# Expert weights in one transfer per matrix, ids and gate weights loaded straight into their integer tile

## The chip, the cores and the metric

One core of one Trainium2 chip runs the whole program. The metric is the device time in microseconds (us) of one launch. Lower is better. Weights and constants may be laid out on the host beforehand; that is not in the time.

## The reference

A long convolution by FFT is followed by a two-level mixture of experts. `x` has the shape (8, 5056, 128) and `h` (5056, 128).

```python
Yf = np.fft.rfft(x, n=2*S, axis=1) * np.fft.rfft(h, n=2*S, axis=0)[None]
y = np.fft.irfft(Yf, n=2*S, axis=1)[:, :S, :]          # 8 x 5056 x 128
x = y.reshape(40448, 128)
g_idx = argmax(x @ w_group)                            # 4 groups
e_idx = argmax(xg @ w_expert[g])                       # 4 experts in each
out[tok] = g_w * e_w * (relu(x[tok] @ w1[g, e]) @ w2[g, e])
```

`w1` is 16 matrices of 128 x 1024 and `w2` 16 matrices of 1024 x 128, all float32. Each row of `x` goes through exactly one expert, and its result is multiplied by the two softmax weights of the choice.

## The kernel before, in words

The first part of the program, up to about 545 us, is the convolution: a Fourier transform in two factors, a product with the transformed `h`, and the way back, in three rounds over the batches. The rows that come out are gated and scattered by GpSimd (POOL) into an array in device memory, `srt`, sorted by expert. A row of `srt` has 130 words: 128 values, the token's id as an integer, and its gate weight.

From about 590 us on the experts run in blocks. A block `j` is 512 rows of one expert, and from the block numbers `T0` and `H0` on 384 and 256 rows, for the rests that the experts leave. Blocks up to `NW_MIN` stand straight in the program, woven with the rest of the convolution (`weave`, lists `main` and `steps`); behind them come three chains of blocks under conditions (`ffn_chain`, `ffn_last`), because their number depends on the routing. For the inputs measured these chains hold 11 blocks of 512 rows, 10 of 384 and 9 of 256.

What a block needs is fetched two blocks ahead by SyncE (SP), all on one queue that works in order. `ffn_x(j)` (from L1265) issues five transfers for a block: four of 32 columns each of the sorted rows into `xr`, and a fifth with the two last columns (id and weight). `ffn_w(j)` (from L1305) issues the expert's weights in four pieces of 128 x 512, in the order 0, 2, 1, 3. Pieces 0 and 1 are the halves of `w1`, L1319; pieces 2 and 3 the halves of `w2`, L1321. In `w2` a partition's 512 words come from four rows of 128 words that lie apart in memory. A transfer into a buffer first waits until the last reader of that buffer is done. In the chains, `again` gives block `j` the buffers of block `j - 2`.

Each piece of weights is split into a high part (a cast on ScalarE, ACT, L1330) and a rest (a subtraction on VectorE, DVE, L1331); from `T0` on the rest of piece 3 is computed on POOL. `ffn_turn` (L1338) transposes the rows on DVE (L1346) and then copies ids and weights from the end of `xr` into the tile `ids` (L1348). `ffn_prep_x` splits the transposed rows with the same lines 1330 and 1331. `mm1` (L1393 to L1395) multiplies by `w1` in three products (high by high, low by high, high by low); `relu` and a second split into `h..h` and `h..l` follow (ACT L1398, DVE L1399). `mm2` (L1411 to L1413) multiplies by `w2`. `out_evac` (L1416) and `out_store` (transpose on TensorE, PE, L1427; product with the gate weight on DVE, L1431, into `orow`) bring the rows back, and `scatter_out` (L1464) has POOL send them to the output by id. `keep_ids` (L1479, L1480) copies a chain block's ids and weights into `lids` at the block's end, because the next block, not this one, stores its rows.

`PLAN` sets at which step of a block each of these is issued. For blocks of 256 rows, with four steps, it reads:

```python
HB: [(0, 0, 1), (0, 0, 2), (1, 0, 3), (1, 1, "t"), (2, 1, "x"), (2, 1, 0), (2.5, 0, "s"), (3, 0, "o"), (3, 0, "w")],
```

An entry is the step, the block counted from the present one, and what is done: a number is a piece of weights to split, "t" the turn, "x" the split of the rows, "s" the store, "o" the scatter, "w" the fetch of weights for two blocks ahead. So in step 1 the present block's piece 3 is split (on POOL) and the next block's rows are turned, and in step 2 the next block's rows and its piece 0 are split. The inverse transform of the last round runs beside the first blocks: `side` loads its data with L723 (`zm`) and L730 (`zt`) on the same SP queue.

Of the kernel before, what the change touches and what calls it, by code (L numbers as in the profile page):

```python
# [9 lines left out]
F32 = mybir.dt.float32  # L10
F32R = mybir.dt.float32r
BF16 = mybir.dt.bfloat16
I32 = mybir.dt.int32
# [6 lines left out]
B, S, D = 8, 5056, 128  # L20
# [5 lines left out]
NE, NF = 16, 1024  # L26
# [14 lines left out]
T0, H0 = 1000, 2000  # L41
# [186 lines left out]
def width(j):  # L228

    return BLK if j < T0 else TB if j < H0 else HB  # L230
# [6 lines left out]
class Kernel:  # L237
# [1027 lines left out]
    def ffn_x(self, j):  # L1265
        nc = self.nc
        tab, k = self.entry(j)
        w = width(j)
        T = w // 128
        rb = nc.sync.value_load(  # L1270
            tab[0:1, 2 * k + 1:2 * k + 2], min_val=0, max_val=NR // BLK - 1 if j < T0 else NR - w
        )
        again = self.again(j)
        if again:
            xr = again["xr"]
        elif j > 0:
            xr = self.fx.tile([128, w + 2 * T], F32, name=f"xr{w}", bufs=2)
        else:
            xr = self.cx.tile([128, w + 2 * T], F32, name="xr0", bufs=1)

        def rows(p, c):
            if j < T0:
                return self.srt.rearrange("(b t p) c -> p b t c", p=p, t=w // p)[:, bass.ds(rb, 1), :, c]
            return self.srt[bass.ds(rb, w), c].rearrange("(t p) c -> p t c", p=p).unsqueeze(1)

        parts = [
            (xr[i:i + SQ, 0:w].rearrange("p (t c) -> p t c", c=SQ), rows(SQ, slice(i, i + SQ))) for i in range(0, D, SQ)
        ]
        parts.append((xr[:, w:w + 2 * T].rearrange("p (t c) -> p t c", c=2), rows(128, slice(D, D + 2))))
        for out, src in parts:  # L1290
            ins = nc.sync.dma_start(out=out.unsqueeze(1), in_=src)
            if j < NC:
                k = 0 if j < N0 else 1 if j < NA else 2
                self.join(f"ids{k}", ins)
                for i in range(k + 1, 3):
                    self.free_of(ins, f"scatter_idx{i}")
                self.free_of(ins, "fill")
        ids = again["ids"] if again else self.cp.tile([128, 4, 2], I32, name="ids", bufs=8)[:, 0:T]
        self.blk[j] = dict(ids=ids, xr=xr, T=T, n=w)

    def again(self, j):
# [3 lines left out]
    def ffn_w(self, j, pieces=(0, 2, 1, 3)):  # L1305
        nc, a = self.nc, self.a
        tab, k = self.entry(j)
        e = nc.sync.value_load(tab[0:1, 2 * k:2 * k + 1], min_val=0, max_val=NE - 1)
        w1 = a["moe_w1"].rearrange("g e d f -> d (g e) f")
        w2 = a["moe_w2"].rearrange("g e (f p) d -> p (g e) f d", p=128)  # L1310
        for q in pieces:
            if self.again(j):
                t = self.again(j)[q]
            elif j > 0 or q == 3:
                t = self.fx.tile([128, 512], F32, name=f"wr{width(j)}", bufs=12 if j < T0 else 8)
            else:
                t = self.xt[(0, 2, 1).index(q)]
            if q < 2:
                nc.sync.dma_start(out=t.unsqueeze(1), in_=w1[:, bass.ds(e, 1), q * 512:(q + 1) * 512])  # L1319
            else:  # L1320
                nc.sync.dma_start(  # L1321
                    out=t.rearrange("p (f d) -> p f d", d=D).unsqueeze(1),
                    in_=w2[:, bass.ds(e, 1), q * 4 - 8:q * 4 - 4, :],
                )
            self.blk[j][q] = t

    def split(self, pair, src, w, eng=None):
        nc = self.nc
# [9 lines left out]
    def ffn_turn(self, j):  # L1338
        nc = self.nc
        s = self.blk[j]  # L1340
        n = s["n"]
        if (j, "x") in self.kept:
            t = self.cx.tile([128, W], F32, name="xturn0", tag="zt", bufs=2)[:, 0:n]
        else:
            t = self.fx.tile([128, BLK], F32, name="xturn", bufs=1)[:, 0:n]
        nc.vector.transpose(out=t, in_=s["xr"][:, 0:n])  # L1346
        s["turned"] = t
        nc.vector.tensor_copy(  # L1348
            out=s["ids"], in_=s["xr"][:, n:n + 2 * s["T"]].bitcast(I32).rearrange("p (t c) -> p t c", c=2)
        )  # L1350

    def ffn_prep_w(self, j, q):
        other = self.nc.gpsimd if j >= T0 and q == 3 and j not in (T0, H0) else None
# [121 lines left out]
    def keep_ids(self, j):  # L1475
        nc = self.nc
        s = self.blk[j]
        T = s["T"]
        nc.vector.tensor_copy(out=self.lids[:, 0:T, 0:1], in_=s["ids"][:, :, 0:1])  # L1479
        nc.vector.tensor_copy(out=self.lids[:, 0:T, 1:2].bitcast(F32), in_=s["ids"][:, :, 1:2].bitcast(F32))  # L1480

    def no_rows(self):

# [326 lines left out]
```

## Time and profile before

| what | value |
|---|---|
| runs timed | 3 |
| median, lowest, highest | 1655.28, 1654.49, 1656.99 us |
| the profiled execution's own time | 1650.14 us |
| its span, first to last instruction | 1648.4 us |
| PE busy in the span | 1585.1 us (96%) |
| DVE busy | 1321.2 us (80%) |
| ACT busy | 1030.5 us (63%) |
| POOL busy | 771.6 us (47%) |

Times in the profile count from the first instruction. "SPq" is SP's transfer queue; the duration there is that of issuing, not of the transfer. In a timeline the bracket behind a row says how long the engine stood idle before it and what ended that idle time. Instructions of one engine overlap a little in these rows, since each is shown from its start to the end of its writes; the step from one start to the next is what an instruction costs its engine.

### The profile page before, as it was taken

What the parts mean: (1) busy time and instruction counts of PE and PEld (TensorE: products, weight loads), DVE (VectorE), ACT (ScalarE), POOL (GpSimd) and SP (SyncE); (2) the same over time, 40 slices, a digit from 0 to 9 for tenths busy, and PEclk for the clock granted to TensorE, in tenths of its full rate; (3) what the DMA queues carried; (4) which work ended last, traced back from release to release, by engine and by line L of the source; (5) the groups of instructions that cost most, each with busy time, mean ns of one, the idle gap of its engine ahead of it and who ended that gap; (6) DMA issues with size and microseconds to landing.
All of it is one profiled execution on the core that took longest, in us unless ns stands there. A gap on an engine that the chain in (4) does not pass through costs nothing. (4 is left out here: it accounts for less than half of the span.)

```text
span 1648.4 us, 48424 instructions
## 1 busy us (share of the span) xinstructions
PE 1585.1 (96%) x16432; PEld 1242.0 (75%) x16432; DVE 1321.2 (80%) x2938; ACT 1030.5 (63%) x2286; POOL 771.6 (47%) x742
## 2 busy tenths in 40 slices
PE   8998999989999989999999999999999999999997
PEld 8676856568666647887787777788888878879986
DVE  6654699875788886888887888888898888888887
ACT  5554544544455545666666666677777776767775
POOL 1453234352565653254555555354665654234544
PEclk9999999999999989999999999999999999999999
DMA  7797778979799988666666655658866787556666
GB/s 212 225 279 238 227 246 269 289 232 237 222 292 302 286 218 177 180 182 174 178 180 171 158 140 143 153 155 224 198 172 172 190 199 185 137 129 162 162 163 158
DMA packets 493295, 330.30 MB, mean 200 GB/s; under 512 B 257052, under 2 KB 436769, under 8 KB 493016
## 3 DMA queue, kind: packets, MB, share of 16 engines
q1 hardware_dynamic: 472408, 285.11, 65.3%
q0 software_dynamic: 20608, 41.79, 7.4%
q8 instruction: 136, 2.23, 0.6%
q14 instruction: 143, 1.17, 0.2%
HBM read 230.41 MB, written 96.86 MB: 199 GB/s over the span
## 5 line engine op out<-in xcount | busy, mean ns | idle before, releaser
L877 POOL DMA_INDIRECT srt<-rw,pos x320 | 342.6, 1071 | 333.9 <-DVE y L551 67.0
L1464 POOL DMA_INDIRECT out<-orow,at x176 | 193.0, 1097 | 263.0 <-ACT at L1462 207.7
L551 DVE TENSOR_TENSOR y<-pp,hg 128x768 f32<-128x768 f32 (+1 forms) x120 | 103.3, 861 | 53.8 <-ACT hg L541 33.6
L1464 POOL DMA_INDIRECT out<-orow,sids x92 | 90.6, 985 | 117.5 <-DVE orow L1431 83.8
L611 ACT COPY zs<-pp 128x768 f32<-128x768 f32 (+1 forms) x118 | 85.4, 723 | 56.5 <-PE pp L601 37.7
L601 PE MATMUL pp<-y,cg 64*64 64x384 f32 (+1 forms) x1472 | 113.8, 440 | 4.9 <-DVE rw L994 2.8
L533 PE MATMUL pp<-st,cg 64*64 64x192 f32 (+1 forms) x1556 | 114.5, 404 | 2.9 <-PE pp L601 1.4
L1398 ACT ACTIVATE h0h<-px 128x512 fp32r<-128x512 f32 (+1 forms) x109 | 64.0, 588 | 82.2 <-PE px L1395 82.2
L766 ACT COPY yT<-py 128x474 f32<-128x474 f32 (+1 forms) x96 | 44.4, 515 | 105.0 <-PE py L759 105.0
L551 DVE TENSOR_TENSOR m<-pp,hg 128x768 f32<-128x768 f32 (+1 forms) x120 | 103.0, 859 | 0.0
L446 DVE TENSOR_TENSOR st<-pp,odd 128x320 f32<-128x320 f32 x90 | 43.8, 487 | 71.0 <-ACT odd L445 70.5
L1399 DVE SCALAR_TENSOR_TENSOR h2l<-px,h2h 128x512 fp32r<-128x512 f32 (+1 forms) x112 | 75.4, 673 | 30.6 <-ACT h2h L1398 26.9
L1399 DVE SCALAR_TENSOR_TENSOR h0l<-px,h0h 128x512 fp32r<-128x512 f32 (+1 forms) x109 | 73.3, 672 | 30.7 <-ACT h0h L1398 30.4
L533 PEld LDWEIGHTS pp<-st,cg 64*64 64x64 f32 x1556 | 59.4, 133 | 44.9 <-issue 29.5
L1399 DVE SCALAR_TENSOR_TENSOR h3l<-px,h3h 128x512 fp32r<-128x512 f32 (+1 forms) x111 | 74.6, 672 | 21.7 <-ACT h3h L1398 20.5
L601 PEld LDWEIGHTS pp<-y,cg 64*64 64x64 f32 x1472 | 56.6, 133 | 43.0 <-issue 29.1
L745 PE MATMUL py<-ig,zm 126*64 126x79 f32 x2048 | 82.1, 236 | 5.1 <-DMA zm<-zd 5.1
L585 POOL TENSOR_TENSOR y<-y,m 128x512 f32<-128x512 f32 x40 | 50.9, 1276 | 76.8 <-DVE m L573 42.0
L745 PEld LDWEIGHTS py<-ig,zm 126*64 126x64 f32 x2048 | 73.9, 138 | 17.1 <-issue 11.0
L1398 ACT ACTIVATE h3h<-px 128x512 fp32r<-128x512 f32 (+1 forms) x111 | 65.2, 587 | 31.2 <-PE px L1395 27.5
L1398 ACT ACTIVATE h2h<-px 128x512 fp32r<-128x512 f32 (+1 forms) x112 | 65.7, 587 | 18.8 <-PE px L1395 12.8
L1398 ACT ACTIVATE h1h<-px 128x512 fp32r<-128x512 f32 (+1 forms) x111 | 65.3, 588 | 18.6 <-PE px L1395 16.6
(474 smaller groups left out, 5051.7 us busy)
## 6 DMA issues: line engine op xcount, KB each, us to landing
wr<-in_moe_w SPq DMA_DIRECT2D x373, 256.0 KB
zm<-zd SPq DMA_DIRECT2D x64, 378.0 KB
zd<-zs SPq DMA_DIRECT2D x62, 384.0 KB
cg<-in_c_g SPq DMA_DIRECT2D x102, 224.0 KB
xr<-srt SPq DMA_DIRECT2D x284, 64.0 KB
xt<-in_x SPq DMA_DIRECT2D x82, 160.0 KB
hg<-hd SPq DMA_DIRECT2D x80, 128.0 KB
zd<-zs SPq DMA_DIRECT2D x39, 256.0 KB
```

The costliest lines, as they stand in the source:

```text
L446: nc.vector.tensor_tensor(out=all_st[:, 0:2 * HALF, d], in0=even, in1=odd, op=ALU.add)
L533: nc.tensor.matmul(px[c * 64:c * 64 + 64, b, to], lhsT=k, rhs=data[:, of], start=begin, stop=i == len(steps) - 1 or p == 0 and i == 1, til ...
L551: self.mark["v"] = nc.vector.tensor_tensor(out=t[:, :, 0:w].rearrange("p t (r u d) -> p t r u d", r=2, u=nu), in0=taken(px, part).unsqueez ...
L585: self.mark["v"] = (nc.gpsimd if r == 0 else nc.vector).tensor_tensor(out=y[:, :, 0:w], in0=y[:, :, 0:w], in1=m[:, :, 0:w], op=ALU.add)
L601: nc.tensor.matmul(pz[c][h:h + 64, 0:w], lhsT=wt[c * 64:c * 64 + 64, k + h:k + h + 64], rhs=y[c * 64:c * 64 + 64, part, 0:w], start=part = ...
L611: self.mark["s"] = nc.scalar.copy(out=z[:, 0:n, 0:w], in_=pp[:, 0:n, 0:w])
L745: nc.tensor.matmul(pys[q][c:c + 64, col(n, u)], lhsT=zms[q][:, n % QB, k:k + 64], rhs=self.ig[:, 0:NH], start=n % QB == 0 and u == 0, stop ...
L766: nc.scalar.copy(out=self.yT[:, k:k + QB * c1], in_=pys.pop(q)[:, 0:QB * c1])
L877: ins = self.nc.gpsimd.indirect_dma_start(out=self.srt, out_offset=bass.IndirectOffsetOnAxis(ap=k["pos"][0:p, j:j + 1], axis=0), in_=k["rw ...
L1398: self.mark["s"] = nc.scalar.activation(out=hh, in_=p, func=AF.Relu)
L1399: nc.vector.scalar_tensor_tensor(out=hl, in0=p, scalar=0.0, in1=hh.bitcast(F32), op0=ALU.max, op1=ALU.subtract)
L1464: ins = self.nc.gpsimd.indirect_dma_start(out=self.a["out"], out_offset=bass.IndirectOffsetOnAxis(ap=ids, axis=0), in_=o, in_offset=None, ...
```

## The change

- `w2` is laid out on the host so that each expert's matrix is 128 rows of 1024 words, a row for each partition, as `w1` already was.
- Each matrix of a block is fetched by one transfer into one tile of 128 x 1024, so that a partition gets 4096 bytes in one piece: two transfers a block where there were four. The first is issued where piece 0 was, the second where piece 2 was. Block 0 keeps its four.
- The fifth transfer of `ffn_x` goes straight into the tile `ids`, which has 10 buffers instead of 8, or, in the chains, the buffer of the block three before. The copy in `ffn_turn` is gone.
- `keep_ids` copies ids and weights in one instruction instead of two.

```diff
@@ ffn_x @@
-            xr = self.fx.tile([128, w + 2 * T], F32, name=f"xr{w}", bufs=2)
+            xr = self.fx.tile([128, w], F32, name=f"xr{w}", bufs=2)
...
+        if again is None:
+            ids = self.cp.tile([128, 4, 2], I32, name="ids", bufs=10)[:, 0:T]
+        else:
+            ids = self.blk[j - 3]["ids"] if j - 3 in self.blk and self.again(j - 1) else None
+            if ids is None:
+                ids = self.cp.tile([128, 4, 2], I32, name="ids", bufs=10)[:, 0:T]
...
-        parts.append((xr[:, w:w + 2 * T].rearrange("p (t c) -> p t c", c=2), rows(128, slice(D, D + 2))))
+        parts.append((ids, rows(128, slice(D, D + 2)).bitcast(I32)))
...
-        ids = again["ids"] if again else self.cp.tile([128, 4, 2], I32, name="ids", bufs=8)[:, 0:T]
@@ ffn_w @@
-        w2 = a["moe_w2"].rearrange("g e (f p) d -> p (g e) f d", p=128)
+        w = [a["moe_w1"].rearrange("g e d f -> d (g e) f"), a["moe_w2"].rearrange("e p f -> p e f")]
         for q in pieces:
...
-            if q < 2:
-                nc.sync.dma_start(out=t.unsqueeze(1), in_=w1[:, bass.ds(e, 1), q * 512:(q + 1) * 512])
...
+            elif q % 2 == 0:
+                if self.again(j):
+                    t = self.again(j)["w", q]
+                else:
+                    t = self.fx.tile([128, 1024], F32, name=f"wr{width(j)}", bufs=6 if j < T0 else 4)
+                nc.sync.dma_start(out=t.unsqueeze(1), in_=w[q // 2][:, bass.ds(e, 1)])
+                self.blk[j]["w", q] = t
+                self.blk[j][q], self.blk[j][q + 1] = t[:, 0:512], t[:, 512:1024]
@@ ffn_turn @@
-        nc.vector.tensor_copy(
-            out=s["ids"], in_=s["xr"][:, n:n + 2 * s["T"]].bitcast(I32).rearrange("p (t c) -> p t c", c=2)
-        )
@@ keep_ids @@
-        nc.vector.tensor_copy(out=self.lids[:, 0:T, 0:1], in_=s["ids"][:, :, 0:1])
-        nc.vector.tensor_copy(out=self.lids[:, 0:T, 1:2].bitcast(F32), in_=s["ids"][:, :, 1:2].bitcast(F32))
+        nc.vector.tensor_copy(out=self.lids[:, 0:T], in_=s["ids"])
@@ kernel @@
+    feed["moe_w2"] = feed["moe_w2"].reshape(NE, NF // 128, 128, D).transpose(0, 2, 1, 3).reshape(NE, 128, NF // 128 * D)
```

## Rows read from the trace of the kernel before

**Rows 1.** Busy time of each engine in stretches of the span (the windows view).

```profile
core 0: us, PE busy (x) PEld busy (x) DVE busy (x) ACT busy (x) POOL busy (x), PEclk, DMA share, GB/s
...
1050.00:1200.00 150.00, 150.00 (x689) 124.10 (x688) 132.60 (x280) 111.71 (x263) 83.31 (x80) 1.00 0.74 192
...
1489.00:1579.00 90.00, 88.59 (x515) 85.08 (x514) 77.78 (x184) 68.31 (x139) 42.21 (x40) 1.00 0.60 156
1579.00:1640.00 61.00, 54.28 (x430) 52.04 (x428) 55.77 (x122) 41.48 (x85) 28.46 (x27) 1.00 0.73 189
```

**Rows 2.** The group of the ids copy on DVE, window 1489 to 1579 us.

```profile
L1348 DVE COPY ids<-xr 128x6 int32<-128x6 int32 x10 | 1.3, 131 | 0.0
```

**Rows 3.** The same group, window 1579 to 1640 us.

```profile
L1348 DVE COPY ids<-xr 128x4 int32<-128x4 int32 x9 | 8.5, 942 | 0.0
```

**Rows 4.** Timeline of all engines inside one block of 256 rows.

```profile
1606.93 0.60 ACT L1398 ACTIVATE h2h<-px 128x512 fp32r<-128x512 f32 x1
...
1607.03 0.43 DVE L1346 STREAM_TRANSPOSE xturn<-xr 128x256 f32<-128x256 f32 x1
1607.11 1.30 POOL L1331 TENSOR_TENSOR w3l<-wr,w3h 128x512 fp32r<-128x512 f32 x1 [1.18 <-ACT w3h L1330]
...
1607.38 1.05 DVE L1348 COPY ids<-xr 128x4 int32<-128x4 int32 x1
...
1607.49 0.41 ACT L1330 CAST x1h<-xturn 128x256 fp32r<-128x256 f32 x1
...
1607.81 0.61 ACT L1330 CAST w0h<-wr 128x512 fp32r<-128x512 f32 x1
...
1608.35 0.68 DVE L1399 SCALAR_TENSOR_TENSOR h2l<-px,h2h 128x512 fp32r<-128x512 f32 x1
...
1608.95 0.41 DVE L1331 TENSOR_TENSOR x1l<-xturn,x1h 128x256 fp32r<-128x256 f32 x1
1609.02 0.28 PE L1393 MATMUL px<-x1h,w0h 128*128 128x256 f32 x1
1609.28 0.68 DVE L1331 TENSOR_TENSOR w0l<-wr,w0h 128x512 fp32r<-128x512 f32 x1
...
1610.02 0.38 PE L1394 MATMUL px<-x1h,w0l 128*128 128x256 f32 x1 [0.71 <-DVE w0l L1331]
...
1610.24 0.28 PE L1395 MATMUL px<-x1l,w0h 128*128 128x256 f32 x1
1610.36 0.28 PE L1393 MATMUL px<-x1h,w0h 128*128 128x256 f32 x1
```

**Rows 5.** Timeline of PE, blocks of 256 rows: first and last such wait.

```profile
1589.04 0.39 PE L1394 MATMUL px<-x0h,w0l 128*128 128x256 f32 x1 [0.66 <-DVE w0l L1331]
...
1638.96 0.39 PE L1413 MATMUL pz<-h3l,w3h 128*128 128x256 f32 x1 [0.86 <-DVE h3l L1399]
```

**Rows 6.** Timeline inside a block of 384 rows: POOL's split beside DVE.

```profile
1524.22 1.29 POOL L1331 TENSOR_TENSOR w3l<-wr,w3h 128x512 fp32r<-128x512 f32 x1 [3.91 <-ACT w3h L1330]
...
1524.31 0.56 DVE L1431 TENSOR_TENSOR orow<-ptr,lids 128x384 f32<-128x384 f32 x1
```

**Rows 7.** Timeline of SP's queue, blocks of 256 rows (start us, us).

```profile
1608.52 0.38 SPq L1321 DMA_DIRECT2D wr<-in_moe_w  x1
1609.85 2.54 SPq L1291 DMA_DIRECT2D xr<-srt  x5
1613.22 0.36 SPq L1319 DMA_DIRECT2D wr<-in_moe_w  x1
```

**Rows 8.** Timeline of DVE, the copy that ends a block of 256 rows.

```profile
1610.89 0.15 DVE L1479 COPY lids<-ids 128x2 int32<-128x2 int32 x1
```

**Rows 9.** Timeline of SP's queue beside the inverse transform.

```profile
627.60 0.37 SPq L1319 DMA_DIRECT2D wr<-in_moe_w  x1
...
629.84 2.18 SPq L723 DMA_DIRECT2D zm<-zd  x2
```

**Rows 10.** Timeline of PE, the same place.

```profile
637.98 1.85 PE L745 MATMUL py<-ig,zm 126*64 126x79 f32 x24 [2.12 <-DMA zm<-zd]
```

More of the change, by code (lines that the diff above doesn't have):

```diff
@@ L1276, in ffn_x @@
         elif j > 0:
-            xr = self.fx.tile([128, w + 2 * T], F32, name=f"xr{w}", bufs=2)
+            xr = self.fx.tile([128, w], F32, name=f"xr{w}", bufs=2)
         else:
-            xr = self.cx.tile([128, w + 2 * T], F32, name="xr0", bufs=1)
+            xr = self.cx.tile([128, w], F32, name="xr0", bufs=1)
         def rows(p, c):
@@ L1308, in ffn_w @@
         e = nc.sync.value_load(tab[0:1, 2 * k:2 * k + 1], min_val=0, max_val=NE - 1)
-        w1 = a["moe_w1"].rearrange("g e d f -> d (g e) f")
-        w2 = a["moe_w2"].rearrange("g e (f p) d -> p (g e) f d", p=128)
+        w = [a["moe_w1"].rearrange("g e d f -> d (g e) f"), a["moe_w2"].rearrange("e p f -> p e f")]
         for q in pieces:
[L1312 to L1317, printed above, removed]
-            if q < 2:
-                nc.sync.dma_start(out=t.unsqueeze(1), in_=w1[:, bass.ds(e, 1), q * 512:(q + 1) * 512])
[L1320 to L1323, printed above, removed]
-                )
-            self.blk[j][q] = t
+            c = slice(q % 2 * 512, q % 2 * 512 + 512)
+            if j == 0:
+                t = self.xt[(0, 2, 1).index(q)] if q < 3 else self.fx.tile([128, 1024], F32, name="wr512", bufs=6)[:, c]
+                nc.sync.dma_start(out=t.unsqueeze(1), in_=w[q // 2][:, bass.ds(e, 1), c])
+                self.blk[j][q] = t
+            elif q % 2 == 0:
[6 more added lines that the diff above has]
+                self.blk[j][q], self.blk[j][q + 1] = t[:, 0:512], t[:, 512:1024]
     def split(self, pair, src, w, eng=None):
@@ L1347, in ffn_turn @@
         s["turned"] = t
-        nc.vector.tensor_copy(
-            out=s["ids"], in_=s["xr"][:, n:n + 2 * s["T"]].bitcast(I32).rearrange("p (t c) -> p t c", c=2)
-        )
     def ffn_prep_w(self, j, q):
```

## The prediction

> **What bounds the kernel now.** I read the busy times by stretch first, because a share over the whole span hides that the limit changes. While the experts run woven with the convolution, PE has no idle time: 150.00 of 150.00 us between 1050 and 1200 us, at a granted clock of 1.00; in the chain of 384 rows it is 88.59 of 90.00 [rows 1]. There DVE and the transfers have room, and nothing taken from them can move the end. In the blocks of 256 rows, from 1579 to 1640 us, PE is busy for only 54.28 of 61.00 us and DVE for 55.77 [rows 1]: the one stretch where DVE sets the pace.
>
> Next I asked the groups of line L1348, the instruction that the change removes. In blocks of 384 rows the ids copy takes 131 ns [rows 2]. In blocks of 256 rows a smaller copy takes 942 ns, 8.5 us in nine [rows 3]. The timeline says why: POOL's split of piece 3 runs from 1607.11 to 1608.41, and the copy that starts at 1607.38 ends at 1608.43, together with it; h2l follows at 1608.35 only [rows 4]. The transpose beside the same split is not held. In blocks of 384 rows the plan lets the copy come after the split.
>
> What PE pays is in the same timeline. L1394 needs w0l, and it starts 1.00 us after the L1393 before it (1609.02 to 1610.02), where neighbours follow each other after 0.12 (1610.24 to 1610.36) [rows 4]; so a block loses 0.88 us. There are seven such waits on w0l in the chain behind a long copy, the first at 1589.04, and in the last block it is the wait on h3l that stands for them, 0.86 us [rows 5]. One block takes (1610.02 - 1589.04) / 3 = 6.99 us [rows 4, 5].
>
> **The change part by part.** *The ids copy on DVE.* It is removed in every block. In blocks of 512 and 384 rows it is about 0.13 us [rows 2] beside a PE that has no gap to give back [rows 1]: nothing. In blocks of 256 rows the chain on DVE moves up. The transpose starts at 1607.03 and the copy 0.35 later; without it, the next one, h2l, must wait for ACT's h2h, ready at 1606.93 + 0.60 = 1607.53, so it starts at about 1607.55 instead of 1608.35 [rows 4]. Then x1l follows 0.60 later and w0l 0.33 after that, as now: 1608.48 instead of 1609.28. Their other inputs are there: x1h at 1607.49 + 0.41 = 1607.90, w0h at 1607.81 + 0.61 = 1608.42 [rows 4]. The gain is 0.80 us a block, below the 0.88 that PE loses, so PE hardly becomes the limit first; a block would take 6.19 us. Eight blocks pay the long copy now (seven waits and the last): 8 x 0.80 = **6.4 us**. Bounds: 0 if the next instruction is held instead, 8 x 0.88 = 7.0 if PE becomes the limit.
>
> *SP's queue in these blocks.* Between the last weight issue at 1608.52 and the next block's first at 1613.22 lie 4.70 us: five row transfers and the bookkeeping around them [rows 7]. Four weight issues, one each (629.84 - 627.60) / 4 = 0.56 us [rows 9], make a cycle of 4.70 + 3 x 0.56 = 6.4 us without any wait; two make 4.70 + 0.56 = 5.3. The first is above the 6.19 that DVE would allow, the second below. So the two parts need each other: the merged transfers cost and give nothing by themselves here, but without them the queue would take back about 0.2 us a block.
>
> *New waits.* The id transfer now writes into the buffer of the block three before, so it waits for the copy at the end of the block just before it; four row transfers stand ahead of it and the weights behind it. The fifth issue comes at 1609.85 + 4 x 0.51 = 1611.9 [rows 7], the copy is over at 1610.89 + 0.15 = 1611.04 [rows 8]: 0.9 us in hand, cost nothing. If that cover is gone, the weights are late by what is missing. A transfer of a whole matrix waits for both halves of the old one: piece 0 now waits for piece 1's split and piece 2 for POOL's. They are fetched two blocks ahead, and the stretch moves 189 GB/s at a transfer share of 0.73 [rows 1], so 512 KB take some 2 us by an estimate from that row (524 KB / (189 / 0.73)) against more than a block of time: nothing.
>
> *The second copy in `keep_ids`* is one short instruction of 0.15 us [rows 8] at a block's end. Behind it DVE waits for ACT anyway: nothing.
>
> *Longer pieces.* 1024 pieces of 512 bytes and 256 of 2048 a block become 256 of 4096. No row shows PE waiting for weights, so no gain, except where something else stands behind them: at 637.98 PE waits 2.12 us for `zm` [rows 10], which SP issued behind four weight transfers [rows 9]. With two issues fewer, `zm` is asked for 2 x 0.56 = 1.1 us earlier. Bounds: the whole wait, 2.1, with about 1 us for the clock that is granted less after it; below, a loss of 1 us if the larger transfers land ahead of row transfers that are needed sooner. I take **1.1 us**, the value of the rows themselves.
>
> The sum is 6.4 + 1.1 = 7.5 us. The profiled execution took 1650.14 us, so it would take 1642.6; it stands 5.1 us below the median of the three runs. The saving does not depend on that difference, so the median goes from 1655.28 to **1647.8 us**.
>
> **The rivals.** *The hold passes to the split of the rows.* The new x1l at 1608.15 still lies beside POOL's split, which ends at 1608.41 [rows 4]. If it is held to that end, w0l starts at 1608.41 + 0.33 = 1608.74, the gain is 0.54 a block, 8 x 0.54 = 4.3, and with the 1.1 the time is 1649.9 us. For it: x1l reads two tensors in SBUF, and no row of before has such an instruction beside POOL's split. Against it: `orow`, the same kind of instruction with one of its two inputs in PSUM, keeps its 0.56 us beside the split [rows 6]. The Trainium skill ("SBUF — State Buffer", section "Who interferes with whom") names this case: a DVE instruction with two SBUF inputs contends with a GpSimd instruction that reads SBUF, and whoever started first blocks the other for its whole length; by that rule the 1649.9 holds.
>
> *The hold passes to h2l.* It also starts beside the split. If it were held until 1608.41, nothing would be gained on DVE: 1655.28 - 1.1 = 1654.2 us, within 0.2%. Against it: h2l reads PSUM like `orow` in [rows 6].
>
> *The queue becomes the limit: slower.* The id transfer with its new wait stands in SP's queue ahead of the weights. If `keep_ids` is late there by more than the 0.9 us above, or a whole matrix waits so long for its second half that the weights arrive after their first cast is due, the 19 blocks of 384 and 256 rows are late each time. From 7.5 / 19 = 0.4 us a block on the saving is gone; at 0.6 us it is 19 x 0.6 - 7.5 = +3.9, 1659.2 us. Against it: 0.9 us in hand, a queue cycle 0.9 us shorter than the block, and two blocks of lead.
>
> **How the numbers follow.** What a measurement of this kernel can tell from no change is about 0.2%, 3.3 us. Chances: the forecast 0.44, the hold on the row split 0.36, the hold on h2l 0.12, the queue 0.08. The first two lie beyond 3.3 us on the faster side, of which I take off 0.03 for a start that goes the wrong way: faster 0.77, the same 0.15, slower 0.08. The range reaches down from the forecast by the upper bounds (7.0 - 6.4 on DVE, 3.1 - 1.1 at `zm`) and about 1.5 us, the scatter of the three runs: 1643.7. Up, it takes in the hold on the row split with the loss of 1 us at `zm` (1655.28 - 4.3 + 1 = 1652.0) and the same scatter: 1653.5. The last two cases lie outside.
>
> **What the profile after would show.** Right: no L1348; in blocks of 256 rows h2l 0.5 us behind the transpose, w0l about 0.8 us earlier, a block of about 6.2 us, and PE's wait on w0l near 0.1. The row split would have 0.41 us by the forecast and about 0.67 if it is held; h2l 0.68 or some 1.5 by the other rival. SP would issue two weight transfers a block of 0.56 us, and the wait for `zm` would be near 1 us. The stretch from 1050 to 1489 us would keep its length. I am wrong if blocks of 256 rows still take 6.99 us, if PE waits for weights or rows anywhere, or if the end moves by more than that stretch and `zm` explain.

## The result, and the profile after

After took 1638.58 us (median of four runs, 1636.24 to 1639.17); before, run beside it, took 1654.88 (1649.72 to 1656.99). The ratio on record is 0.9916, with a 95% interval from 0.9895 to 0.9938 (the quotient of the two medians, 0.9902, lies in it): **faster by 16.3 us** between the medians, about twice the 7.5 us forecast, and outside the range. The profiled execution of after took 1639.17 us with a span of 1637.5, that of before 1650.14 with 1648.4. So 10.9 us can be followed through the two traces. The other 5.4 us cannot: the profiled run of before is among its quickest, that of after is its slowest, and what the longer runs of before lose in addition no trace shows.

To see where the 10.9 us come from I compared the starts of the row transposes, counting only those of 128x512, which are 70 in both kernels.

| stretch, by the count of the transpose | before, us | after, us | difference |
|---|---|---|---|
| start of the span to the 1st | 597.20 | 598.53 | +1.3 |
| 1st to 4th (the `zm` wait lies here) | 46.91 | 42.95 | -4.0 |
| 4th to 58th (experts and inverse transform) | 689.78 | 689.32 | -0.5 |
| 58th to 62nd (the rests' first blocks are fetched ahead) | 50.19 | 47.04 | -3.1 |
| 62nd to 70th (chain of 512 rows) | 92.64 | 92.65 | 0.0 |
| 70th to the end (384 and 256 rows) | 171.68 | 167.01 | -4.7 |

The +1.3 us is not explained. In the experiments below the same stretch takes from 650.2 to 661.1 us without following the change, so it is more likely scatter.

The busy times of after by stretch, the counterpart of [rows 1] (the columns are the same; the stretches are moved by what was gained ahead of them):

```profile
1050.00:1200.00 150.00, 150.00 (x689) 124.17 (x688) 132.35 (x267) 111.40 (x264) 85.54 (x81) 1.00 0.69 189
1482.50:1572.50 90.00, 88.46 (x514) 84.95 (x513) 76.04 (x162) 68.07 (x140) 42.22 (x40) 1.00 0.63 162
1572.50:1633.00 60.50, 54.99 (x434) 52.53 (x432) 49.78 (x108) 41.62 (x85) 30.31 (x28) 0.99 0.69 193
...
1577.50:1622.50 45.00, 44.73 (x359) 43.31 (x358) 40.34 (x86) 35.09 (x72) 22.42 (x21) 1.00 0.72 197
```

The first two stretches are as before. In the blocks of 256 rows DVE fell from 55.77 of 61.00 us to 49.78 of 60.50, and in the middle of them PE is busy for 44.73 of 45.00 us. For before the view of PE's waits from 1579 us to the end lists eight on w0l, the longest 0.7, and one of 0.9 on h3l; of after it lists these two:

```profile
PE ptr L1427 <- ACT oT L1416: 0.5, 1, 0.5
PE pz L1413 <- DVE h3l L1399: 0.2, 1, 0.2
```

One such block of after, in time, the counterpart of [rows 4] (PEld is PE's loading of the fixed operand ahead of a product):

```profile
1598.77 0.43 DVE L1349 STREAM_TRANSPOSE xturn<-xr 128x256 f32<-128x256 f32 x1
1598.86 1.30 POOL L1334 TENSOR_TENSOR w3l<-wr,w3h 128x512 fp32r<-128x512 f32 x1 [1.18 <-ACT w3h L1333]
...
1599.31 0.69 DVE L1399 SCALAR_TENSOR_TENSOR h2l<-px,h2h 128x512 fp32r<-128x512 f32 x1
...
1599.92 0.53 DVE L1334 TENSOR_TENSOR x1l<-xturn,x1h 128x256 fp32r<-128x256 f32 x1
1600.37 0.68 DVE L1334 TENSOR_TENSOR w0l<-wr,w0h 128x512 fp32r<-128x512 f32 x1
...
1600.79 0.28 PE L1393 MATMUL px<-x1h,w0h 128*128 128x256 f32 x1
...
1601.10 0.19 PEld L1394 LDWEIGHTS px<-x1h,w0l 128*128 128x128 f32 x1 [0.23 <-DVE w0l L1334]
1601.10 0.39 PE L1394 MATMUL px<-x1h,w0l 128*128 128x256 f32 x1
```

The copy is gone, and h2l starts 0.54 us behind the transpose and is not held (0.69). But x1l takes 0.53 us instead of 0.41: it starts beside POOL's split, which ends at 1598.86 + 1.30 = 1600.16, and it ends 0.29 us after that. A block takes (1617.75 - 1592.44) / 4 = 6.33 us between transposes, against 6.99. The busy share of PE hides what is left of the wait: from L1393 to L1394 it still steps 1601.10 - 1600.79 = 0.31 us where neighbours step 0.12, so about 0.19 us a block still goes to w0l.

At the first place the queue of SP now reads (the counterpart of [rows 9]):

```profile
626.96 0.90 SPq L1326 DMA_DIRECT2D wr<-in_moe_w  x2
628.75 1.16 SPq L723 DMA_DIRECT2D zm<-zd  x2
```

`zm` is asked for at 628.75 instead of 629.84, the 1.1 us of the forecast; yet PE no longer waits for it at all, and the stretch is 4.0 us shorter. PE's rows there, in before (the wait of [rows 10] lies between them):

```profile
634.82 1.04 PE L745 MATMUL py<-ig,zm 126*64 126x79 f32 x24
...
639.76 1.79 PE L759 MATMUL py<-igt,zt 64*64 64x158 f32 x24
```

In after:

```profile
636.09 1.86 PE L745 MATMUL py<-ig,zm 126*64 126x79 f32 x48
637.88 1.04 PE L759 MATMUL py<-igt,zt 64*64 64x158 f32 x24
```

And the stretch behind the wait in before, in the columns of [rows 1]; the last but two is the granted clock:

```profile
638.00:641.40 3.40, 3.40 (x48) 2.88 (x48) 0.00 (x0) 0.00 (x0) 0.00 (x0) 0.51 0.22 35
```

PE comes to these products 636.09 - 634.82 = 1.27 us later than in before, and the request went out 1.09 us earlier; together 2.36 us, more than the 2.12 of the wait. With the wait went a second loss: behind it the granted clock was 0.51 for 3.4 us, the lower of its two levels (1.2 GHz), and 24 products of L745 took 1.85 us and those of L759 1.79. In after the clock there is 1.00, 48 products of L745 take 1.86 us and 24 of L759 1.04. That is about 0.9 and 0.75 us, so wait and clock make some 3.8 of the 4.0 us.

The third place was not in the forecast. In before, ACT's timeline there reads:

```profile
1351.36 0.62 ACT L1330 CAST w0h<-wr 128x512 fp32r<-128x512 f32 x1 [2.91 <-DMA wr<-in_moe_w]
...
1351.98 0.59 ACT L1398 ACTIVATE h1h<-px 128x512 fp32r<-128x512 f32 x1
```

And PE's:

```profile
1352.62 0.50 PE L1411 MATMUL ptr<-h1h,w3h 128*128 128x512 f32 x1 [2.20 <-ACT h1h L1398]
```

PE's wait carries the name of h1h. But h1h stood on ACT behind w0h, and w0h stood for a transfer of weights. The queue of SP ahead of that, in before:

```profile
1335.58 2.46 SPq L1291 DMA_DIRECT2D xr<-srt  x5
1338.83 0.36 SPq L1319 DMA_DIRECT2D wr<-in_moe_w  x1
1340.04 3.61 SPq L1291 DMA_DIRECT2D xr<-srt  x5
1343.85 0.39 SPq L1454 DMA_DIRECT2D take<-outd  x1
1345.04 0.38 SPq L1321 DMA_DIRECT2D wr<-in_moe_w  x1
1346.54 1.57 SPq L1319 DMA_DIRECT2D wr<-in_moe_w  x2
```

Here `ffn_ahead` puts the rows and weights of the blocks T0, T0+1, H0 and H0+1 between those of the running blocks, all in one order, and the queue is late. By the semaphores of the trace, the signals on which an instruction waits, the cast of w0h waits for the second transfer of the last row, issued at 1347.76 us; ACT comes to the cast at 1351.36 - 2.91 = 1348.45. In after the transfer for the same cast is the second of the three at 1336.42, issued at 1338.26, 6.8 us ahead of the cast. The queue of after:

```profile
1336.42 2.77 SPq L1326 DMA_DIRECT2D wr<-in_moe_w  x3
1340.58 2.56 SPq L1297 DMA_DIRECT2D xr<-srt  x4
1343.33 2.11 SPq L1297 DMA_DIRECT2D ids<-srt  x1
1345.64 0.39 SPq L1454 DMA_DIRECT2D take<-outd  x1
1347.01 0.94 SPq L1326 DMA_DIRECT2D wr<-in_moe_w  x2
```

The busy times around the cast of w0h, in the columns of [rows 1]. Before (the cast at 1351.36 us) and after (at 1345.10):

```profile
1350.00:1355.00 5.00, 2.80 (x10) 1.32 (x8) 2.99 (x5) 3.64 (x10) 3.91 (x4) 1.00 1.06 300
...
1345.00:1350.00 5.00, 4.99 (x20) 3.33 (x19) 4.96 (x9) 5.00 (x15) 4.04 (x4) 1.00 0.85 208
```

PE is busy for 2.80 of 5.00 us before, and not idle after.

### The profile page after: what moved, and what is told of

Same layout as the page of the kernel before. It is cut to its first block, busy times and chain, and to the rows that moved or that the text cites. A ratio compares the mean times of both kernels' runs of the same rounds, so it can differ in the third digit from the quotient of the medians.

```text
span 1637.5 us, 47586 instructions
## 1 busy us (share of the span) xinstructions
PE 1582.0 (97%) x16432; PEld 1239.5 (76%) x16432; DVE 1309.4 (80%) x2817; ACT 1028.5 (63%) x2286; POOL 771.6 (47%) x742
## 5 line engine op out<-in xcount | busy, mean ns | idle before, releaser
L585 POOL TENSOR_TENSOR y<-y,m 128x512 f32<-128x512 f32 x40 | 50.9, 1275 | 76.1 <-DVE m L573 43.6
L745 PEld LDWEIGHTS py<-ig,zm 126*64 126x64 f32 x2048 | 73.1, 137 | 15.2 <-issue 9.3
L745 PE MATMUL py<-ig,zm 126*64 126x79 f32 x2048 | 81.3, 235 | 3.2 <-DMA zm<-zd 3.2
```

The lines of the kernel that those rows point to most:

```text
L585: self.mark["v"] = (nc.gpsimd if r == 0 else nc.vector).tensor_tensor(out=y[:, :, 0:w], in0=y[:, :, 0:w], in1=m[:, :, 0:w], op=ALU.add)
L745: nc.tensor.matmul(pys[q][c:c + 64, col(n, u)], lhsT=zms[q][:, n % QB, k:k + 64], rhs=self.ig[:, 0:NH], start=n % QB == 0 and u == 0, stop ...
```

## The experiments

They ran on two chips, 12 and 7 by the record, which does not name the chip of the first comparison. `two_ahead`, `two_early`, `two_queues` and `after_dve` are from chip 7, the other eight from chip 12. Before takes 100 us more there than in the first comparison: its medians are 1758.4 and 1758.6 us on chip 12 and 1757.6 on chip 7, in 68 runs that scatter from about 1750 to 1769. Why was not found. Each ratio is therefore taken against before on the same chip and at the same time. The only trace of before, `before_again`, is from chip 12, so where a stretch of the four kernels on chip 7 is set beside those with four issues, two chips are compared. After keeps its advantage on chip 12: `after_again`, the same kernel, has the ratio 0.9890.

A table first, since the experiments are read against each other. "Issues" is what SP issues for the weights of a block. The last three columns are from each kernel's one profiled execution; a block's time is the step between transposes, without the first.

| kernel | issues | ids copy | ratio to before, 95% | 58th to 62nd, us | 70th to end, us | 256-row block, us |
|---|---|---|---|---|---|---|
| before_again | 4 | yes | 1.0018 [0.9995, 1.0040] | 63.0 | 176.9 | 7.1 to 7.9 |
| four_long | 4 | yes | 1.0001 [0.9974, 1.0027] | 58.4 | 176.9 | 6.8 to 7.9 |
| ids_only | 4 | no | 0.9993 [0.9972, 1.0013] | 58.3 | 172.7 | 6.8 (one 6.2) |
| ids_again | 4 | no | 0.9996 [0.9976, 1.0016] | 59.2 | 172.0 | 6.5 to 7.2 |
| copy_first | 4 | moved | 1.0005 [0.9986, 1.0024] | 58.9 | 173.4 | 6.5 to 7.5 |
| two_ahead | 2 in four blocks | yes | 0.9960 [0.9938, 0.9982] | 54.0 | 173.5 | 6.8 (last 7.5) |
| two_early | 2 up to the 512 rows' end | yes | 0.9938 [0.9916, 0.9959] | 53.5 | 175.2 | 6.8 to 7.6 |
| two_queues | 2 on SP, 2 on ACT | yes | 1.0121 [1.0093, 1.0149] | 53.3 | 179.9 | 6.7 to 7.5 |
| two_short | 2 | yes | 0.9924 [0.9898, 0.9949] | 53.4 | 172.1 | 6.8 |
| weights_only | 2 | yes | 0.9936 [0.9912, 0.9961] | 50.9 | 171.4 | 6.7 to 6.9 |
| after_again | 2 | no | 0.9890 [0.9860, 0.9920] | 51.7 | 170.6 | 6.8 (one 6.2) |
| after_dve | 2 | no | 0.9914 [0.9881, 0.9947] | 51.5 | 174.1 | 7.3 |

**The two parts alone.** `ids_only` takes the change of `ffn_x`, `ffn_turn` and `keep_ids`, and leaves the weights as they were.

```diff
-        parts.append((xr[:, w:w + 2 * T].rearrange("p (t c) -> p t c", c=2), rows(128, slice(D, D + 2))))
+        parts.append((ids, rows(128, slice(D, D + 2)).bitcast(I32)))
...
-        nc.vector.tensor_copy(
-            out=s["ids"], in_=s["xr"][:, n:n + 2 * s["T"]].bitcast(I32).rearrange("p (t c) -> p t c", c=2)
-        )
```

> Only the id transfer into its own tile and the single copy in keep_ids; weights in four pieces as before. If the copy that POOL's split holds is what the blocks of 256 rows lose, these blocks go from 6.99 us to about 6.4 (SP's queue with four weight issues sets the pace then), 7 x 0.6 = 4 us in all, near 1650.5 us against 1654.9; the wait for zm at 638 us and the wait on ACT near 1351 us stay. If the whole gain came from the id transfer, it would be near 1639. If the copy did not matter, 1655.

`weights_only` takes the new layout and `ffn_w`, and leaves the ids copy.

```diff
-            if q < 2:
-                nc.sync.dma_start(out=t.unsqueeze(1), in_=w1[:, bass.ds(e, 1), q * 512:(q + 1) * 512])
...
+                nc.sync.dma_start(out=t.unsqueeze(1), in_=w[q // 2][:, bass.ds(e, 1)])
```

> Only the weights: two transfers a block with 4096-byte pieces; the ids copy stays. Theory: the waits near 638 us and 1351 us go (3.9 and 3.1 us in the two profiles), blocks of 256 rows stay at 6.99 us: 7 us less in the profile, and the rest of the 16 us between the medians if that belongs to those two places too, so 1640 to 1648. Rival, that the ids part is all: 1655.

The weights alone carry most of the gain, 0.9936 against 0.9890 for both parts. The ids part alone gives no total that can be told from no change, although its stretch from the 70th transpose on is 4.2 us shorter than in `before_again`; `ids_again`, the same kernel once more, said the same (172.0 us, ratio 0.9996). Those 4.2 us would be a ratio of 0.9976, which the interval of `ids_only` does not exclude.

> Only the id transfer and the single copy in keep_ids, weights in four pieces. In the blocks of 256 rows: SP's queue with four weight issues sets the pace, 6.4 to 6.8 us a block against 6.33 with the whole change, so 2 to 4 us gained in the tail and nothing before it. Rival: the blocks go at 6.33 us, the queue is no limit. The waits near 638 and 1351 us, or their like on this chip, stay.

**Length of the pieces, or number of issues?** `two_short` issues one transfer a matrix but keeps the old layout of `w2`, so its pieces stay at 512 bytes. `four_long` has the new layout and four transfers, of 2048-byte pieces.

```diff
@@ two_short @@
+                    out=t.rearrange("p (f d) -> p f d", d=D).unsqueeze(1), in_=w2[:, bass.ds(e, 1), c0 // D:c1 // D, :]
@@ four_long @@
+                nc.sync.dma_start(out=t.unsqueeze(1), in_=w2[:, bass.ds(e, 1), (q - 2) * 512:(q - 1) * 512])
```

> Two transfers a block, but w2 in its old layout, so eight pieces of 512 bytes a partition. If the gain at 638 us and 1351 us is that SP's queue issues two transfers fewer, this is as fast as weights_only, within 1 us. If it is the length of the pieces, it stays near 1655, at most w1's share of the gain less.

> Four transfers a block, but w2 in the new layout, so pieces of 2048 bytes everywhere. If the number of issues on SP's queue is what counts, it stays within 2 us of 1655 and shows both waits. If the length of the pieces counts, it is as fast as weights_only.

Short pieces in two transfers: 0.9924. Long pieces in four: 1.0001. The layout does nothing that can be measured here; what the weights gain comes with the number of issues.

**The two ends once more**, on chip 12 beside the others: before against itself, and after.

> The kernel before, unchanged, for a trace on the same chip as the runs beside it. Blocks of 256 rows at the pace of the other profile of before (6.99 us) if they are bound by DVE alone; the chip of the first four runs was slower (1758 us for before), and if the chip counts there too, slower.

> The kernel after, unchanged, on the same chip. About 0.99 of before, as in the first comparison; 6.33 us a block of 256 rows.

The ratio came as expected, the block did not: 6.78 us instead of 6.33. Ahead of the transposes of L1427, which wait for ACT's oT, PE steps 0.44 to 0.50 us in these blocks of `after_again`, where after steps 0.12; in `ids_only` it is 0.47 to 0.51. So on chip 12 another wait holds the blocks, with either number of issues. Its cause is open.

**Where do fewer issues pay?** `two_ahead` merges the transfers only for the four blocks that are fetched ahead, `two_early` only for blocks of 512 rows. Both use short pieces and keep the ids copy.

```diff
@@ two_ahead @@
+            if j > 0 and (j in (T0, T0 + 1, H0, H0 + 1)):
@@ two_early @@
+            if j > 0 and (j < T0):
+                if q == 0:
+                    nc.sync.dma_start(out=m.unsqueeze(1), in_=w1[:, bass.ds(e, 1), :])
```

> Before, with the two merged transfers only for the four blocks that are fetched ahead (T0, T0+1, H0, H0+1); all other blocks keep four, and the ids copy stays. Theory (the issues queue up where four blocks are fetched ahead while the chain of 512 rows goes on fetching its own): the place where ACT's w0h waits for its weights in the stretch before the chain of 512 rows is free, 3 us gained where before takes 1655 us and 6 to 8 us where it takes 1758; ratio 0.996 to 0.998; the wait for zm around 640 us keeps its 2 us. Rival (it is the many blocks, each a little): 8 of some 370 issues change nothing, ratio 0.999 to 1.001.

> Before, with the two merged transfers only for blocks of 512 rows; the blocks of 384 and 256 rows, the four fetched ahead among them, keep four, and the ids copy stays. Theory: the zm place gains 2 to 4 us, and the fetch-ahead place gains a part of its share, since half of what stands in the queue there belongs to blocks of 512 rows; ratio 0.995 to 0.998, and the blocks of 256 rows stay as in before (7 us or more). Rival (the gain of two transfers comes from the blocks of 384 and 256 rows): 0.999 to 1.001.

`two_ahead` is as its theory said: 8 issues fewer in the whole program, and 0.9960. `two_early` gained more than I expected (0.9938). Look at the column "58th to 62nd" of the table: the five kernels with four issues everywhere need 58.3 to 63.0 us there, and the seven that take issues off SP, whichever half of them, 50.9 to 54.0. The ranges don't touch. But the stretch has more than one wait in it. ACT's waits for the weights of w0h, from 1425 to 1500 us, tell them apart, in `before_again`, `two_ahead` and `two_early` (in all us, times, longest):

```profile
ACT w0h L1330 <- DMA wr<-in_moe_w: 4.0, 2, 3.5
...
ACT w0h L1342 <- DMA wr<-in_moe_w: 0.6, 1, 0.6
...
ACT w0h L1342 <- DMA wr<-in_moe_w: 2.8, 1, 2.8
```

In the five kernels with four issues everywhere the longest of these waits is 2.4 to 4.0 us. In `two_ahead` it is 0.6, in `two_queues`, `weights_only`, `after_again` and `after_dve` there is none, in `two_short` 1.3; but in `two_early` it stays at 2.8. So the wait that stands at 1351.36 us in the first trace hangs on the issues of the blocks that are fetched ahead, as the theory of `two_ahead` had it, and merging the running blocks' transfers does not bring these weights in time. What `two_early` gains in the stretch lies elsewhere: PE's longest wait behind it, on oT, is 2.7 us there and 3.8 to 5.2 in the five (4.3 in `two_ahead`). That wait does not stand in the first two traces, and its cause is open. A second stretch behaves partly alike, from the 40th to the 58th transpose: four issues in the running blocks 220.5 to 222.5 us, two of them 213.4 to 220.2 (`two_queues` 229.5, see below). In the first comparison that stretch did not change (204.24 and 204.07), and its cause stays open.

**Does it have to be SP?** `two_queues` keeps four transfers, but has ACT issue pieces 1 and 3 on its own queue.

```diff
+            eng, r = (nc.scalar, e2) if j > 1 and q % 2 else (nc.sync, e)
+            if q < 2:
+                eng.dma_start(out=t.unsqueeze(1), in_=w1[:, bass.ds(r, 1), q * 512:(q + 1) * 512])
```

> Before, with its four transfers a block, but pieces 1 and 3 issued by ACT on its own queue. Theory (what costs is the number of issues that stand in order on SP's queue): as good as the merged transfers, ratio 0.991 to 0.995, less what the issues cost ACT: some 2 us if each takes ACT's time where PE waits for it. Rival (what costs is the number of transfers, wherever issued): 0.999 to 1.002. A third way: ACT stands waiting for a buffer to come free before it can issue, and PE waits for ACT: slower, 1.005 and more.

The third way came: 1.0121. ACT stands still for transfers; two rows of its waits from 600 to 1500 us, neither of which stands in `before_again` (in all us, times, longest):

```profile
ACT yT L766 <- DMA wr<-in_moe_w: 25.0, 8, 4.1
ACT h3h L1400 <- DMA xr<-srt: 19.8, 4, 6.9
```

A block of 384 rows takes 9.60 us instead of 8.92. But the stretch from the 58th to the 62nd transpose is as short as with merged transfers, 53.3 us, though the number of transfers is that of before, and ACT does not wait for the weights of w0h there. What made these weights late was the order on SP's queue, not the number of transfers.

**What holds the ids copy?** `copy_first` is before with the ids copy ahead of the transpose, earlier than POOL's split.

```diff
+        nc.vector.tensor_copy(
+            out=s["ids"], in_=s["xr"][:, n:n + 2 * s["T"]].bitcast(I32).rearrange("p (t c) -> p t c", c=2)
+        )
         nc.vector.transpose(out=t, in_=s["xr"][:, 0:n])
```

> The kernel before with the ids copy moved ahead of the transpose, so that it runs before POOL's split begins; it still copies. If POOL's split holds the copy, it takes 0.13 us there instead of 1.05 and the blocks of 256 rows go at the pace of ids_again. If the copy is long for a reason of its own, it stays 1 us long and the blocks stay as before.

The stretch from the 70th transpose on is 3.5 us shorter than in `before_again`, without any change of weights or transfers, and the copy takes 0.30 us in the mean. Two blocks of `before_again` side by side show the rule. POOL's splits:

```profile
1721.06 1.30 POOL L1331 TENSOR_TENSOR w3l<-wr,w3h 128x512 fp32r<-128x512 f32 x1 [1.65 <-ACT w3h L1330]
...
1728.23 1.30 POOL L1331 TENSOR_TENSOR w3l<-wr,w3h 128x512 fp32r<-128x512 f32 x1 [2.03 <-ACT w3h L1330]
```

And the copies on DVE:

```profile
1720.88 0.13 DVE L1348 COPY ids<-xr 128x4 int32<-128x4 int32 x1
...
1728.36 1.19 DVE L1348 COPY ids<-xr 128x4 int32<-128x4 int32 x1
```

The copy that starts 0.18 us ahead of the split is not lengthened; the one that starts 0.13 us behind it lasts until the split ends (1728.36 + 1.19 = 1729.55, the split 1729.53). One copy of `two_queues` that starts 0.03 us behind the split is not held, so the border is not exactly at equal starts. Where two held copies follow each other in `before_again`, the blocks are 7.84 and 7.86 us apart; where two copies escape one after the other in `four_long`, with the same four issues, 6.78. That is also why `weights_only` has short blocks with the copy still in them. The group of the copy over the last eight blocks of `before_again`:

```profile
L1348 DVE COPY ids<-xr 128x4 int32<-128x4 int32 x8 | 7.1, 888 | 0.0
```

And in `weights_only`:

```profile
L1346 DVE COPY ids<-xr 128x4 int32<-128x4 int32 x8 | 1.8, 225 | 0.0
```

There the copy came ahead of the split in seven of eight blocks. What sets which of the two comes first in a series of blocks is not settled: `two_ahead` has four issues in most of these blocks and short blocks too. The two parts of the change thus overlap here: in the profiles each alone frees most of the blocks of 256 rows, and their gains there don't add. In the first trace of before the split starts 0.09 us behind the transpose in block after block, and no copy beside a split escapes.

**Does the hold pass to the split of the rows?** `after_dve` is after with the rest of piece 3 on DVE instead of POOL in these blocks.

```diff
-        other = self.nc.gpsimd if j >= T0 and q == 3 and j not in (T0, H0) else None
+        other = self.nc.gpsimd if H0 > j >= T0 and q == 3 and j != T0 else None
```

> After, with the rest of piece 3 computed on DVE instead of POOL in blocks of 256 rows. If POOL's split is what lengthens the split of the rows there, x1l and x0l of 128x256 take 0.41 us in every block instead of 0.50 to 0.53; if they are long for another reason (ACT writing beside them), they stay at 0.50. DVE gets 0.6 us more a block, so a block gets up to 0.5 us longer and the time stays or grows by up to 4 us against after; against before 0.990 to 0.994.

The groups of the row split over the last nine blocks, in `after_again`:

```profile
L1334 DVE TENSOR_TENSOR x1l<-xturn,x1h 128x256 fp32r<-128x256 f32 x5 | 2.5, 505 | 0.0
...
L1334 DVE TENSOR_TENSOR x0l<-xturn,x0h 128x256 fp32r<-128x256 f32 x4 | 2.0, 503 | 0.0
```

and in `after_dve`:

```profile
L1334 DVE TENSOR_TENSOR x1l<-xturn,x1h 128x256 fp32r<-128x256 f32 x5 | 2.0, 403 | 0.0
...
L1334 DVE TENSOR_TENSOR x0l<-xturn,x0h 128x256 fp32r<-128x256 f32 x4 | 1.6, 404 | 0.0
```

Without POOL's split it takes 0.40 us in every block; with it 0.50 in the mean, 0.53 in the seven blocks of nine in which it lies beside the split. The block gets 0.5 us longer, since DVE now carries the split, as expected. The hold by POOL is shown.

## Why the prediction was wrong

**The step that failed** is this one: "No row shows PE waiting for weights, so no gain, except where something else stands behind them". There was such a row, under another name: PE's 2.20 us at 1352.62 are given to h1h, and h1h is late because it stands behind w0h on ACT, which waits 2.91 us for `wr`. I asked PE's waits for weights and did not ask ACT, which is the engine that reads them first. It cost 3.1 us in the profile; on chip 12 the same wait of ACT is 2.4 to 4.0 us, and the weights, the part put at "no gain" but for `zm`, carry most of the change. That SP's queue was late at this place could be read from before: I costed the queue only in the blocks of 256 rows, and not where four blocks more are put into it. The price was off there too. I took 0.56 us an issue, from weights that stand one behind the other; where `ffn_ahead` issues them one by one, before takes 1.14 us from one to the next:

```profile
1330.92 0.34 SPq L1319 DMA_DIRECT2D wr<-in_moe_w  x1
1332.06 0.38 SPq L1321 DMA_DIRECT2D wr<-in_moe_w  x1
```

**The `zm` term was mis-sized.** 1.1 us were forecast, with 3.1 as the upper bound; the stretch gained 4.0. The request was 1.1 us earlier as worked out, but PE also came 1.27 us later, so the wait of 2.12 us vanished entirely; by these numbers some 1.0 us of it would have been left, as forecast, had PE come as early as in before. How much of that is luck is open, since the 1.3 us lost ahead of the 1st transpose are not explained. And the clock was under-priced: the bound allowed about 1 us for it, the rows give about 1.6. In the traces of chips 12 and 7 PE does not wait for `zm` at this place, so no experiment tests this.

**The DVE term: right in kind, about 4.6 us instead of 6.4.** The copy was held by POOL, it is gone, and h2l is not held, as forecast. The first rival came with it, the hold on the row split. By it the forecast of 0.80 us a block becomes 0.54; measured 6.99 - 6.33 = 0.66, since the next instruction starts 0.45 us after x1l and 0.21 after the split's end, not 0.33. The Trainium skill ("SBUF — State Buffer", section "Who interferes with whom") had the kind of it right, and for more than I used it for: whoever starts first blocks the other, and the trace shows the copy escape at 0.18 us ahead and be held at 0.13 behind. In size it fits less well: held for the whole rest of the split, x1l was to take about 0.67 us, and it took 0.53. A further slip was the count: eight blocks were charged, but the time from the last transpose to the end is 13.43 us before and 13.41 after, so the last block gives nothing. Seven times 0.66 is 4.6.

**PE as the next limit** is near, but not reached. PE is busy for 44.73 of 45.00 us at 6.33 us a block, and still loses 0.19 us of each to w0l; without that a block would take 6.33 - 0.19 = 6.14 us by these rows. So it is the hold on x1l, not PE, that kept the block from the forecast of 6.19.

**Right:** nothing is gained in the chains of 512 and 384 rows; the new wait of the id transfer and the wait of a whole matrix for both halves cost nothing that PE's waits show; the slower rival did not come. "The two parts need each other" was not borne out: with four issues the blocks of 256 rows reach 6.78 us in `ids_only`, as with two in `after_again`. Whether four issues would have allowed the 6.33 of the first comparison is not shown, since no kernel reaches it on chips 12 and 7 for more than one block.

The sum by the traces is 4.0 + 0.5 + 3.1 + 4.7 - 1.3 = 11.0 us, against 10.9 between the spans. The 5.4 us that only the medians show stay without a trace of the slower runs.

## What to carry to other kernels

Follow a wait past the name it carries: where PE waits for an engine, ask what that engine waited for just before, and what stands behind the late instruction on it. On one queue that works in order the number of issues is a cost of its own: look for the places where a burst of extra transfers is put between the regular ones, and cost the queue there, not in the steady loop. And when two edits each remove the same delay, measure each alone before adding their gains.

## What was not expected of the hardware

- The length of the contiguous pieces did not matter: with two transfers a block, 512-byte pieces of `w2` took 1744.05 us and 4096-byte pieces 1745.56, though the transfers' share is near 0.7 in most stretches.
- A DVE copy of 128x4 takes 0.13 us or 1.19, depending on whether it starts 0.18 us before or 0.13 us after a POOL subtraction of 1.30 us.
- The same program took 1655 us in the first comparison and 1758 on chips 12 and 7, at granted clocks of 0.992 and 0.986 in the two profiles of before. That the chip makes the difference is likely, but the record does not name the first one.
- After PE had stood for 2.12 us, the granted clock was 0.51 for 3.4 us, which cost about 1.6 us more. After it had stood for 2.20 us at 1352.62, the clock stayed at 1.00.
